# Scores of the remaining queries from six products instead of eight, with padded low keys filled by transfers and a new order of the work

## The chip, the core and the metric

The kernel runs on one core of a Trainium2 chip. The metric is the device time of one launch in microseconds (us); of the kernel before there are three runs: 879.49, 881.54 and 882.21 us, with the median 881.54. One more execution was recorded by the profiler: it took 880.19 us, 1.35 us less than that median, and 878.4 us of it are the span that the trace shows. Five engines work side by side on such a core: PE multiplies matrices (with PEld, its loading of weights, beside it), DVE, ACT and POOL work on vectors, and SP here only issues transfers (DMAs). Each takes its instructions in the order in which the program lists them, and waits at an instruction until what it reads is there and what it overwrites is free.

## What is computed

Thresholded attention over 8 batches of 8 heads with 576 positions of 64 numbers each, and behind it a gated MLP for each batch:

```python
scores = 0.125 * q @ k.T                          # 576 x 576 for each batch and head
thresh = scores.max(-1) - tau
attn = exp(where(scores >= thresh, scores, -1e9) - scores.max(-1))
x = (attn / attn.sum(-1)) @ v                     # heads side by side: 576 x 512 for each batch
h = gelu(x @ w_in)                                # 576 x 1024
u, g = h[..., :512], layernorm(h[..., 512:]) * g_ln
out = x + (u * (w_sg @ g + b_sg)) @ w_out
```

The large products are wanted at close to float32 precision. The kernel splits an operand into a high part (rounded to PE's fast format, fp32r) and a low part (the rest), and adds up high times high, low times high and high times low.

## The kernel before

**Pairs.** The 8 heads of a batch are worked in pairs, 64 rows of the 128 partitions for each head: 32 pairs, numbered n. Pairs 0 to 3 (the first batch, `whole_s`) take scores from unsplit operands. Pairs 4 to 31 (`by_rows`), with which the change deals, go by the split:

- `q_load` brings the queries of both heads (a tile rq), `q_scale` (POOL) multiplies them by 0.125, `q_hi` (ACT) writes the high part (qhi), `q_lo` (POOL) leaves the low part in rq. Four transfers (L472) build for each head h a tile qst[h]: the head's high queries in its own 64 rows, its low queries in the other 64.
- `k_load` brings the keys (rk), `k_hi` (ACT, L439) writes the high keys (khi, in the buffer that held qhi), four transfers (L456, `k_place`) put the high keys of head h into both halves of a tile ks[h], of which there are two sets for odd and even pairs.
- `k_lo` (POOL, L448) subtracts the high keys from the keys, once for each head, straight into klz[h]: a tile with the low keys of head h in its own 64 rows and zeros, written once at the start, in the other 64. There is one klz[0] and one klz[1] for all pairs.

So the product of qst[h] with ks[h] over 128 rows is high times high plus low times high, and that with klz[h] is high times low. `scores` (L546) makes a tile of 128 queries by 576 keys from them: two halves of 288 keys, two products each. A pair has nine tiles: four for each head, and between them one of the remaining 64 queries of both heads (i == NM, the tail tile). In the tail tile's columns of qst[0] the queries of head 1 are zeros, and the reverse; it sums both heads, four products for each half, eight in all.

**What follows a tile.** DVE takes the row maxima (L555, nm), POOL the threshold (L561), ACT the exponentials (L582, p or, for the tail tile, pm), DVE selects and sums (L589) and transposes blocks (L599, turned). When a pair is through, PE multiplies with the values v (L755). The inverse sums go out and back by transfers (L661 to L669, ld and ir); DVE scales (L762).

**MLP.** When four pairs are through, that batch's MLP products (L849) are mixed in between the scores of the next batch; the last batch's stand alone at the end. ACT changes its function table (L1164) whenever it goes from exponentials to gelu or back.

**Order.** Every step is put into a list by `at` or `put`. The table ORDER, a long string of numbers, says in which sequence the list is issued; each engine gets its instructions in that sequence. There is one such string for the kernel, written into it; FIRST_BANKS says which banks of PSUM the products use.

Of the kernel before, what the change touches and what calls it, by code (L numbers as in the profile page):

```python
# [37 lines left out]
    "G+zxNBj+qyd?xk4XF6bg3cEKMr!WF#YQ<7|Mnd5LDxOZmkA!nFj20*>?*+kq%I)dF{WXR6^uzQ0!7M6735qCfe0@#I>ZY^pz?wD&dREonuC{a2G)g_yc"
    "{o5FxPeAHEQ2{o3M`wJxiD>t-$B=V&pW&;GJ^3UyM<po5lG(6=egn`T(#9`7gMJ%T3<l4P8SuK<?{t(QNQO@gJXG%Hx@6;M+&gaA<`bTnYmSc__VF?1D"
    "zn6+rUO1ME%bcc1ix^%*sxCuDl-kH!T|-kO*dHJGCT&(62oQsoEDpqH^?zb&;<{sQ-(O7@(DzPZ(+zxM9_-K0e6K5VES#u&mV<tI?wNd{lzmb`9cf}0N"  # L40
    "p4F9<bCcHIfueyy1eOsr!QKzRjRd;sohNHrPc8;rK$UG%pxdIR4=FL5CE{Pyd4Z0Ta_D#f;Vr)L>GCWn=O|4}+VNE-HgnIEz#dvQP0OroyRK{JN1dojM"
    "ZYMxgkDH6ZaYs5sU2DW*lLV)HXVziu<dBre10mAEZmx6T&*!n{)a^oHsxOrK%vG;-Zfl{p{6MV;yU%}tC63vzURQMfdV#*kncv-uShB*>V~#r({Q-)JE"
# [70 lines left out]
Q = 32  # L113
# [9 lines left out]
def tile_threshold_attention_gated_mlp(  # L123
# [283 lines left out]
    def attention(n, g0):  # L407
# [34 lines left out]
        def k_part(h):  # L442
            return (S + front, 0) if h else (S, front)
# [728 lines left out]
```

## Time and profile before

| | before |
|---|---|
| runs, us | 879.49, 881.54, 882.21 (median 881.54) |
| profiled execution, us | 880.19, span 878.4 |
| busy in the span, us | PE 841.2, DVE 707.3, ACT 592.6, POOL 585.6 |
| granted clock of PE, mean | 0.996 |
| transfers | 117.00 MB, 46.5% of the 16 DMA engines' time |

The span has three stages. Until about 95 us the weights are split and pairs 0 to 3 run. From there to about 820 us attention of pairs 4 to 31 and the MLPs of the first seven batches run mixed. The last 58 us are the MLP of the last batch. Of a busy PE one must know that its matmuls overlap: a product of 288 columns is shown with about 0.3 us, but they start 0.13 us apart.

### The profile page before, as it was taken

How to read it: one execution, taken by the hardware profiler on the slowest of the kernel's cores; microseconds unless marked ns; L12 is line 12 of the kernel's file. 1: busy time of each engine (PE TensorE's matmuls, PEld its weight loads, DVE VectorE, ACT ScalarE, POOL GpSimd, SP SyncE). 2: the span in 40 equal slices, each digit the busy share in tenths (PEclk: the TensorE clock that was granted, in tenths of full speed). 3: DMA queues.
4: the chain of work that ended last, by engine and by line, in shares of the span. 5: the costliest groups of instructions: out<-in, count | busy, mean ns of one | idle time of the engine just before them, and what ended most of it. 6: DMA issues, size and time to landing. Idle time of an engine off the chain costs nothing.

```text
span 878.4 us, 30879 instructions
## 1 busy us (share of the span) xinstructions
PE 841.2 (96%) x12642; PEld 745.7 (85%) x12642; DVE 707.3 (81%) x1444; ACT 592.6 (67%) x1045; POOL 585.6 (67%) x965
## 2 busy tenths in 40 slices
PE   7998999989989999999999999999999999999998
PEld 4555789988878988898789988899889898999898
DVE  8998979888789889878888888898997888987111
ACT  6987986455865778755787657865677557784152
POOL 4875677575775576746776477755777667764477
PEclk9999999999999999999999999999999999999999
DMA  6642343475255464465555465356545545622101
GB/s 235 215 126 67 100 125 100 131 203 144 70 151 160 133 187 130 122 165 138 155 138 140 140 190 159 75 161 177 150 132 147 139 129 143 184 80 78 47 8 54
DMA packets 73024, 117.00 MB, mean 133 GB/s; under 512 B 10161, under 2 KB 32689, under 8 KB 72882
## 3 DMA queue, kind: packets, MB, share of 16 engines
q1 hardware_dynamic: 72882, 115.02, 46.5%
q8 instruction: 99, 1.62, 0.8%
q14 instruction: 43, 0.35, 0.1%
HBM read 70.55 MB, written 9.57 MB: 91 GB/s over the span
## 4 chain that ended last, share of the span: by engine, by line
PE 46%; POOL 13%; DVE 8%; ACT 5%; issue 5%; DMA 5%; SPq 1%; POOLq 0%; DVEq 0%; ACTq 0%
PE all_banks L849 29%; PE all_banks L546 9%; PE all_banks L755 7%; POOL ot L1056 3%; DVE nm L555 2%; DVE turned L599 2%; DVE p L589 2%; POOL klz L448 2%; ACT L1164 2%; DMA v<-in_vR 1%; POOL gl L1023 1%; POOL rq L465 1%; ACT p L582 1%; POOL vv L950 1%; POOL nm L561 1%
## 5 line engine op out<-in xcount | busy, mean ns | idle before, releaser
L582 ACT ACTIVATE p<-all_banks,nm 128x576 f32<-128x576 f32 x256 | 184.1, 737 | 110.4 <-DVE nm L555 109.3
L589 DVE SCALAR_TENSOR_TENSOR p<-all_banks,nm,p 128x576 f32<-128x576 f32 x256 | 202.1, 807 | 41.9 <-ACT p L582 25.1
L555 DVE TENSOR_REDUCE nm<-all_banks 128x1 f32<-128x576 f32 x288 | 207.0, 741 | 30.5 <-PE all_banks L546 22.2
L546 PE MATMUL all_banks<-ks,qst 128*128 128x288 f32 x560 | 164.2, 312 | 12.5 <-DVE p L589 7.4
L599 DVE STREAM_TRANSPOSE turned<-p 128x576 f32<-128x576 f32 x224 | 165.6, 756 | 2.2 <-PE all_banks L755 2.1
L546 PE MATMUL all_banks<-klz,qst 128*128 128x288 f32 x560 | 155.3, 296 | 3.3 <-POOL klz L448 2.7
L755 PE MATMUL all_banks<-turned,v 32*64 32x144 f32 x8064 | 147.1, 286 | 2.7 <-issue 1.7
L561 POOL TENSOR_TENSOR nm<-columns,nm 128x1 f32<-128x1 f32 x288 | 53.0, 192 | 133.7 <-DVE nm L555 112.8
L755 PEld LDWEIGHTS all_banks<-turned,v 32*64 32x64 f32 x8064 | 127.5, 130 | 16.3 <-issue 11.9
L546 PEld LDWEIGHTS all_banks<-ks,qst 128*128 128x128 f32 x560 | 105.1, 188 | 31.2 <-DVE p L589 18.4
L1164 ACT ACT_TABLE_LOAD x89 | 114.2, 1283 | 1.6
L849 PE MATMUL all_banks<-wsh,z 128*128 128x288 f32 (+2 forms) x512 | 110.7, 298 | 0.6 <-DVE p L589 0.6
L546 PEld LDWEIGHTS all_banks<-klz,qst 128*128 128x128 f32 x560 | 105.4, 188 | 5.2 <-POOL klz L448 4.0
L448 POOL TENSOR_TENSOR klz<-rk,khi 64x576 fp32r<-64x576 f32 x56 | 79.9, 1427 | 15.4 <-PE all_banks L546 8.4
L849 PEld LDWEIGHTS all_banks<-wsh,z 128*128 128x128 f32 x512 | 84.0, 188 | 2.7 <-DVE p L589 1.1
L849 PE MATMUL all_banks<-gh,woh 128*128 128x288 f32 (+2 forms) x256 | 75.9, 301 | 0.6 <-issue 0.2
L849 PE MATMUL all_banks<-xh,wih 128*128 128x288 f32 (+2 forms) x256 | 74.5, 298 | 0.6 <-DVE pm L589 0.4
L849 PE MATMUL all_banks<-gh,wol 128*128 128x288 f32 (+2 forms) x256 | 75.1, 298 | 0.0
L849 PE MATMUL all_banks<-xh,wil 128*128 128x288 f32 (+2 forms) x256 | 74.7, 298 | 0.0
L849 PE MATMUL all_banks<-xl,wih 128*128 128x288 f32 (+2 forms) x256 | 74.6, 295 | 0.0
L849 PE MATMUL all_banks<-wsl,z 128*128 128x288 f32 (+2 forms) x256 | 73.9, 296 | 0.0
L849 PE MATMUL all_banks<-gl,woh 128*128 128x288 f32 (+1 forms) x240 | 71.2, 300 | 0.0
(142 smaller groups left out, 1827.9 us busy)
## 6 DMA issues: line engine op xcount, KB each, us to landing
v<-in_vR SPq DMA_DIRECT2D x112, 288.0 KB
ks<-khi SPq DMA_DIRECT2D x112, 144.0 KB
rq<-in_qT SPq DMA_DIRECT2D x28, 320.0 KB
qst<-rq SPq DMA_DIRECT2D x56, 160.0 KB
qst<-qhi SPq DMA_DIRECT2D x56, 160.0 KB
rk<-in_kT SPq DMA_DIRECT2D x28, 288.0 KB
ir<-ld SPq DMA_DIRECT2D x56, 144.0 KB
out_T<-ot SPq DMA_DIRECT2D x56, 144.0 KB
```

The source lines that it names most:

```text
L448: nc.gpsimd.tensor_tensor(klz[h][rows, 0:w], st["k"][rows, o:o + w], st["kh"][rows, o:o + w], ALU.subtract)
L465: nc.gpsimd.tensor_tensor(lo.bitcast(F32R), lo, st["qh"][:, :wq], ALU.subtract)
L546: nc.tensor.matmul(sc[:, a, 0:HALF], w, x, start=(j == 0), stop=(j == len(terms) - 1))
L555: nc.vector.tensor_reduce(nmax, st["s", h, i][:, :, 0:HALF], AX.XY, ALU.max, negate=True)
L561: nc.gpsimd.tensor_tensor(thr, toff, st["nm", h, i], ALU.subtract)
L582: nc.scalar.activation(target(h, i), st["s", h, i][:, :, 0:HALF], AF.Exp, bias=st["nm", h, i])
L589: nc.vector.scalar_tensor_tensor(dst, st["s", h, i][:, :, 0:HALF], st["thr", h, i], dst, ALU.is_ge, ALU.mult, accum_out=st["l"][:, c:c + 1])
L599: nc.vector.transpose(st["turned"][:, :, o:o + Q], st["p", i][:, c0:c0 + S].rearrange("p (k x) -> p k x", x=Q))
L755: nc.tensor.matmul(st["accs"][g // 2][hs, g % 2, 0:W], st["v"][rows, o:o + D], st["turned"][rows, k, h * W:(h + 1) * W], start=(k == 0), s ...
L849: nc.tensor.matmul(st["acc"], *term(j), start=(j == 0), stop=(j == n - 1))
L1056: return lambda: nc.gpsimd.tensor_tensor(o(), o(), x[b, m][:, ts_], ALU.add)
L1164: tables[kind]()
```

## The change

The tail tile is made from three products for each half instead of four. The first two are high times high and low times high of head 0 and of head 1 (ks[0], ks[1]), as before. The two with zero padding are replaced by one: a new tile kl holds the low keys of both heads, each in its 64 rows, and a new tile qtail the high queries of the tail columns of both heads. Since the columns of one head are zeros in the other's rows, one product over 128 rows gives both.

- `k_lo` is one POOL subtraction over 128 rows into kl, instead of two over 64 rows into klz[0] and klz[1].
- klz[0] and klz[1], which the eight other tiles still need, are filled by two transfers from kl on SP's queue (`k_place_lo`, L449 of the kernel after).
- qtail is an ACT copy of 128 columns of qhi (`q_tail`, L453).
- kl and qtail are single buffers. kl of pair n+1 can be written when pair n's tail tile is through, and so can qtail. khi overwrites the buffer of qhi, so that khi of a pair now comes behind its qtail.
- The values of pairs 0 to 3 are loaded into a free part of the tile that later holds their transposed probabilities (tag pt), instead of a tile of their own.
- The host puts the tail columns of both heads last, and klz[1] is 576 wide instead of 640.
- ORDER and FIRST_BANKS are new: all engines get their work in another sequence. ACT has 79 changes of table in it, where it had 89 (the one at the start not counted).

```diff
--- before.py
+++ after.py
@@ -31,76 +31,77 @@
 ORDER = (
...
 FIRST_BANKS = (
...
@@ -226,7 +227,9 @@
     wt2 = cpool.tile([TAIL + 2, S], F32R, name="wt2")
 
     qst = [[cpool.tile([P, KW], F32R, name=f"qst{h}{i}") for i in range(2)] for h in range(2)]
-    klz = [cpool.tile([P, (S, KW)[h]], F32R, name=f"klz{h}") for h in range(2)]
+    klz = [cpool.tile([P, S], F32R, name=f"klz{h}") for h in range(2)]
+    kl = cpool.tile([P, S], F32R, name="kl")
+    qtail = cpool.tile([P, P], F32R, name="qtail")
     pm = cpool.tile([P, KW], F32, name="pm")
     nc.vector.memset(pm, 0.0)
 
@@ -417,9 +420,7 @@
         front = 0 if by_rows else TAIL
 
         def load(name, src, w):
-            if name == "v":
-                pool, width, tag = raws, KW, "v"
-            elif whole_s:
+            if whole_s:
                 pool, width, tag = {"q": ((raws, KW, "raw1"), (raws, S, "raw0"), (kpool, S, "ks01"), (xpool, S, "xl6")),
                                     "k": ((kpool, KW, "ks10"), (kpool, KW, "hi"), (kpool, KW, "ks11"), (xpool, KW, "xh6"))}[name][n]
             else:
@@ -439,22 +440,24 @@
                 nc.scalar.activation(st[name + "h"][:, :w], st[name][:, :w], AF.Copy)
             return f
 
-        def k_part(h):
-            return (S + front, 0) if h else (S, front)
-
-        def k_lo(h):
-            def f():
-                rows, (w, o) = slice(h * D, (h + 1) * D), k_part(h)
-                nc.gpsimd.tensor_tensor(klz[h][rows, 0:w], st["k"][rows, o:o + w], st["kh"][rows, o:o + w], ALU.subtract)
-            return f
+        def k_lo():
+            nc.gpsimd.tensor_tensor(kl, st["k"][:, 0:S], st["kh"][:, 0:S], ALU.subtract)
+
+        def k_place_lo(h):
+            def f():
+                rows = slice(h * D, (h + 1) * D)
+                nc.sync.dma_start(klz[h][rows].bitcast(F32), kl[rows].bitcast(F32))
+            return f
+
+        def q_tail():
+            nc.scalar.activation(qtail, st["qh"][:, MAIN:KW], AF.Copy)
 
         def k_place(h):
             def f():
-                w, o = k_part(h)
                 st["ks", h] = kpool.tile([P, (S, KW)[h]], F32R, tag=f"ks{h}{n % 2}", name=f"ks{n}_{h}")
                 for d0 in (0, D):
-                    nc.sync.dma_start(st["ks", h][d0:d0 + D, 0:w].bitcast(F32),
-                                      st["kh"][h * D:(h + 1) * D, o:o + w].bitcast(F32))
+                    nc.sync.dma_start(st["ks", h][d0:d0 + D, 0:S].bitcast(F32),
+                                      st["kh"][h * D:(h + 1) * D, 0:S].bitcast(F32))
             return f
 
         def q_scale():
@@ -468,13 +471,8 @@
             def f():
                 for h in range(2):
                     r0 = (h ^ swap) * D
-                    c0 = 0 if by_rows else h * TAIL
-                    nc.sync.dma_start(q[h][r0:r0 + D, c0:c0 + wq].bitcast(F32), st[name][h * D:(h + 1) * D, 0:wq].bitcast(F32))
-            return f
-
-        def q_zeros():
-            for h in range(2):
-                nc.gpsimd.memset(q[h][:, (S, 0)[h]:(KW, TAIL)[h]].bitcast(F32), 0.0)
+                    nc.sync.dma_start(q[h][r0:r0 + D].bitcast(F32), st[name][h * D:(h + 1) * D].bitcast(F32))
+            return f
 
         wq = KW if by_rows else S
         w = wq + (n == 0)
@@ -487,17 +485,22 @@
             at_k()
         else:
             at("q_hi", lead, hi_part("q", wq))
+            at("q_tail", lead, q_tail)
             at("q_lo", lead, q_lo)
             at("q_place", lead, q_place("qh", 0))
             at("q_place_lo", lead, q_place("q", 1))
-            if not by_rows:
-                at("q_zero", lead, q_zeros)
             at_k()
             at("k_hi", lead, hi_part("k", S + front))
+            at("k_lo", lead, k_lo)
             for h in range(2):
-                at("k_lo", lead, k_lo(h))
+                at("k_place_lo", lead, k_place_lo(h))
             at("k_place0", lead, k_place(0))
             at("k_place1", lead, k_place(1))
+
+        def rest_of(a, c0, w):
+            if ("half", a) not in st:
+                st["half", a] = ptp.tile([P, (NB * P, NB * 2 * W)[a]], F32, tag=("v4", "pt")[a], name=f"pt{n}_{a}")
+            return st["half", a][:, c0:c0 + w]
 
         def load_repeated(c):
             def f():
@@ -507,11 +510,15 @@
                 nc.sync.dma_start(st["v"][:, cs], vR[n - WHOLE_SCORES, :, cs])
             return f
 
+        def load_values():
+            st["v"] = rest_of(1, 9 * SPLIT[1][1], KW)
+            nc.sync.dma_start(st["v"], vP[b, hp])
+
         if by_rows:
             for c in range(NB * P // S):
                 at("v_load", g0, load_repeated(c))
         else:
-            at("v_load", g0, load("v", vP[b, hp], KW))
+            at("v_load", g0, load_values)
 
         def both_scores(i):
             def f():
@@ -529,19 +536,17 @@
             def f():
                 sc = st["s", h, i] = two_banks(f"s{n}_{h}_{i}")
                 for a in range(2):
-                    rows = slice(h * D, (h + 1) * D)
-                    qo, ko = h * 2 * TAIL + i * P, a * HALF
+                    cs, ks = slice(i * P, (i + 1) * P), slice(a * HALF, (a + 1) * HALF)
                     if whole_s and i == NM:
                         for g in range(2):
                             rows, qo = slice(g * D, (g + 1) * D), (1 - g) * MAIN
                             nc.tensor.matmul(sc[rows, a, 0:HALF], st["q"][rows, qo:qo + TAIL],
-                                             st["k"][rows, TAIL + ko:TAIL + ko + HALF], start=True, stop=True)
+                                             st["k"][rows, TAIL + a * HALF:TAIL + (a + 1) * HALF], start=True, stop=True)
                         continue
                     if i < NM:
-                        parts_of = [(h, q[h][:, qo:qo + P], ko)]
+                        terms = [(q[h][:, cs], x[:, ks]) for x in (st["ks", h], klz[h])]
                     else:
-                        parts_of = [(g, w, ko + g * front) for g, w in enumerate((q[0][:, MAIN:KW], q[1][:, 0:P]))]
-                    terms = [(w, x[:, o:o + HALF]) for g, w, o in parts_of for x in (st["ks", g], klz[g])]
+                        terms = [*((q[g][:, cs], st["ks", g][:, ks]) for g in range(2)), (qtail, kl[:, ks])]
                     for j, (w, x) in enumerate(terms):
                         nc.tensor.matmul(sc[:, a, 0:HALF], w, x, start=(j == 0), stop=(j == len(terms) - 1))
             return f
@@ -679,11 +684,6 @@
                         rows, c0 = slice(h * D, (h + 1) * D), h * TAIL
                         nc.scalar.activation(r[rows, MAIN:S], tp[rows, 1, c0:c0 + TAIL], AF.Copy)
             return f
-
-        def rest_of(a, c0, w):
-            if ("half", a) not in st:
-                st["half", a] = ptp.tile([P, (NB * P, NB * 2 * W)[a]], F32, tag=("v4", "pt")[a], name=f"pt{n}_{a}")
-            return st["half", a][:, c0:c0 + w]
 
         def unit(h, a):
             w = SPLIT[a][1]
@@ -1124,7 +1124,7 @@
             ends = np.zeros((d, groups, 2, half), q.dtype)
             ends[:, :, e] = x[:, rest[e]].reshape(d, groups, half)
             ends = ends.reshape(d, P)
-            qT[i, 2 * j + e, :, :wide] = np.concatenate([ends, x[:, body[e]]] if e else [x[:, body[e]], ends], axis=1)
+            qT[i, 2 * j + e, :, :wide] = np.concatenate([x[:, body[e]], ends], axis=1)
     vv = v.reshape(b, h // 2, 2, s, d)
     vm = np.ascontiguousarray(vv[:, :, :, :main].reshape(b, h // 2, 2, main // P, P, d).transpose(0, 1, 4, 3, 2, 5))
     vt = np.zeros((b, h // 2, 2, s - main, 2, d), v.dtype)
```

The order of the instructions shows the change at the transition from pair 17 to pair 18. In its names a number behind the name is that of the pair, with the head behind it or behind an underscore; the number behind the last underscore only tells buffers apart. qst00 and qst10 are qst of head 0 and 1 for even pairs, qst01 and qst11 those for odd ones; all_banks is PSUM.

On PE, pair 17's tail tile before:

```order
L546 MATMUL all_banks_93<-ks17_0_6247,qst01_136 128x288
L546 MATMUL all_banks_93<-klz0_139,qst01_136 128x288
L546 MATMUL all_banks_93<-ks17_1_6252,qst11_138 128x288
L546 MATMUL all_banks_93<-klz1_140,qst11_138 128x288
L546 MATMUL all_banks_93<-ks17_0_6247,qst01_136 128x288
L546 MATMUL all_banks_93<-klz0_139,qst01_136 128x288
L546 MATMUL all_banks_93<-ks17_1_6252,qst11_138 128x288
L546 MATMUL all_banks_93<-klz1_140,qst11_138 128x288
```

and after:

```order
L551 MATMUL all_banks_93<-ks17_0_6214,qst01_136 128x288
L551 MATMUL all_banks_93<-ks17_1_6211,qst11_138 128x288
L551 MATMUL all_banks_93<-kl_141,qtail_142 128x288
L551 MATMUL all_banks_93<-ks17_0_6214,qst01_136 128x288
L551 MATMUL all_banks_93<-ks17_1_6211,qst11_138 128x288
L551 MATMUL all_banks_93<-kl_141,qtail_142 128x288
```

Two products of the tile are gone. Behind it come other products, and then the tiles (0, 3) and (1, 3) of the pair, in both kernels.

On POOL, where pair 18's low keys are made (L561 and L566 are thresholds of pair 17, L950 a step of the MLP), before:

```order
L943 TENSOR_SCALAR bn3_3_6663<-bn3_3_6663 128x1
L448 TENSOR_TENSOR klz0_139<-rk18_6379,khi18_6490 64x576
L950 TENSOR_TENSOR vv3_3_6602<-vv3_3_6602,g_bc_108 128x512
L561 TENSOR_TENSOR nm17_1_3_6696<-columns_105,nm17_1_3_6696 128x1
L561 TENSOR_TENSOR nm17_0_3_6688<-columns_105,nm17_0_3_6688 128x1
L448 TENSOR_TENSOR klz1_140<-rk18_6379,khi18_6490 64x576
L619 TENSOR_SCALAR l17_6383<-l17_6383 128x9
```

and after:

```order
L566 TENSOR_TENSOR nm17_1_2_6613<-columns_105,nm17_1_2_6613 128x1
L444 TENSOR_TENSOR kl_141<-rk18_6208,khi18_6625 128x576
L950 TENSOR_TENSOR vv3_0_6347<-vv3_0_6347,g_bc_108 128x512
L566 TENSOR_TENSOR nm17_1_3_6686<-columns_105,nm17_1_3_6686 128x1
L566 TENSOR_TENSOR nm17_0_3_6678<-columns_105,nm17_0_3_6678 128x1
L963 TENSOR_TENSOR z3_0_6690<-vv3_0_6347,z3_0_6690 128x512
```

One subtraction stands where there were two, and it needs only the tail tile of pair 17 to be through, no longer the tiles (0, 3) and (1, 3).

On SP's queue, the transfers that put pair 18's keys into place (v4_17 are pieces of pair 17's values; rq19 and rk19 are loads of the next pair), before:

```order
L456 DMA ks18_1_6620<-khi18_6490 64x576 x2
L1059 DMA out_T<-ot2_1_1_6335 128x288
L1059 DMA out_T<-ot2_1_0_6227 128x288
L507 DMA v4_17_6625<-in_vR 128x576
L456 DMA ks18_0_6627<-khi18_6490 64x576 x2
L507 DMA v4_17_6625<-in_vR 128x576 x2
L431 DMA rk19_6816<-in_kT 128x576
```

and after:

```order
L459 DMA ks18_1_6666<-khi18_6625 64x576 x2
L510 DMA v4_17_6662<-in_vR 128x576
L459 DMA ks18_0_6670<-khi18_6625 64x576 x2
L449 DMA klz1_140<-kl_141 64x576
L449 DMA klz0_139<-kl_141 64x576
L432 DMA rk19_6700<-in_kT 128x576
L510 DMA v4_17_6662<-in_vR 128x576 x2
```

Two transfers that wait for pair 17's last tiles now stand in the queue, ahead of the load of rk19 and of two of the four pieces of pair 17's values.

## Rows read from the trace of the kernel before

**Rows 1.** Page: busy time (share of the span) and instructions of each engine.

```profile
PE 841.2 (96%) x12642; PEld 745.7 (85%) x12642; DVE 707.3 (81%) x1444; ACT 592.6 (67%) x1045; POOL 585.6 (67%) x965
```

**Rows 2.** Windows, mixed stage: busy us (instructions) of each engine, clock, DMA share, GB/s.

```profile
95.00:820.00 725.00, 702.34 (x11750) 640.73 (x11749) 613.93 (x1235) 493.58 (x833) 485.24 (x791) 1.00 0.51 139
```

**Rows 3.** Page, chain of work that ended last: shares of the span.

```profile
PE 46%; POOL 13%; DVE 8%; ACT 5%; issue 5%; DMA 5%; SPq 1%; POOLq 0%; DVEq 0%; ACTq 0%
PE all_banks L849 29%; PE all_banks L546 9%; PE all_banks L755 7%; POOL ot L1056 3%; DVE nm L555 2%; DVE turned L599 2%; DVE p L589 2%; POOL klz L448 2%; ACT L1164 2%; DMA v<-in_vR 1%; POOL gl L1023 1%; POOL rq L465 1%; ACT p L582 1%; POOL vv L950 1%; POOL nm L561 1%
```

**Rows 4.** Waits: us in total, times, longest.

```profile
DVE p L589 <- ACT p L582: 25.1, 36, 1.6
DVE nm L555 <- PE all_banks L546: 22.2, 36, 2.5
PEld all_banks L546 <- DVE p L589: 18.4, 44, 1.3
PEld all_banks L546 <- POOL klz L448: 4.0, 5, 2.2
PE all_banks L546 <- POOL klz L448: 2.7, 3, 2.0
```

**Rows 5.** Timeline of PE, pair 17's tail tile and four products ahead: start us, us, what.

```profile
438.36 0.29 PE L546 MATMUL all_banks<-ks,qst 128*128 128x288 f32 x1
...
439.81 0.30 PE L546 MATMUL all_banks<-klz,qst 128*128 128x288 f32 x1
439.94 0.29 PE L849 MATMUL all_banks<-gh,woh 128*128 128x288 f32 x1
```

**Rows 6.** Groups by line: busy us, mean ns of one, idle before, releasers.

```profile
L546 PE MATMUL all_banks<-ks,qst 128*128 128x288 f32 x560 | 164.2, 312 | 12.5 <-DVE p L589 7.4 <-DVE pm L589 2.1 <-DVE ir L762 1.1
L546 PE MATMUL all_banks<-klz,qst 128*128 128x288 f32 x560 | 155.3, 296 | 3.3 <-POOL klz L448 2.7 <-issue 0.5
L1164 ACT ACT_TABLE_LOAD x89 | 114.2, 1283 | 1.6
L448 POOL TENSOR_TENSOR klz<-rk,khi 64x576 fp32r<-64x576 f32 x56 | 79.9, 1427 | 15.4 <-PE all_banks L546 8.4 <-issue 2.3 <-DMA qst<-rq 1.4
L785 POOL TENSOR_TENSOR xl<-ir,xh 128x576 fp32r<-128x576 f32 x28 | 40.0, 1430 | 11.8 <-ACT xh L780 11.7
L1164 ACT ACTIVATE spare<-columns 128x1 f32<-128x1 f32 x89 | 18.1, 203 | 1.0
L730 ACT ACTIVATE pt<-all_banks 128x128 f32<-128x128 f32 (+1 forms) x20 | 5.5, 276 | 1.0 <-PE all_banks L242 0.8
```

**Rows 7.** Timeline of POOL, pair 18's low keys, and of DVE behind them.

```profile
443.92 1.43 POOL L448 TENSOR_TENSOR klz<-rk,khi 64x576 fp32r<-64x576 f32 x1 [0.65 <-PE all_banks L546]
445.30 1.29 POOL L950 TENSOR_TENSOR vv<-vv,g_bc 128x512 f32<-128x512 f32 x1
446.56 0.33 POOL L561 TENSOR_TENSOR nm<-columns,nm 128x1 f32<-128x1 f32 x2
446.96 1.44 POOL L448 TENSOR_TENSOR klz<-rk,khi 64x576 fp32r<-64x576 f32 x1
...
446.92 0.82 DVE L589 SCALAR_TENSOR_TENSOR p<-all_banks,nm,p 128x576 f32<-128x576 f32 x1 [0.21 <-POOL nm L561]
```

**Rows 8.** Timeline of PE: pair 17's last product with klz, pair 18's first two.

```profile
444.07 0.29 PE L546 MATMUL all_banks<-klz,qst 128*128 128x288 f32 x1
...
449.07 0.29 PE L546 MATMUL all_banks<-ks,qst 128*128 128x288 f32 x1
449.21 0.29 PE L546 MATMUL all_banks<-klz,qst 128*128 128x288 f32 x1
```

**Rows 9.** Issues of the key transfers on SP: ns min/median/max.

```profile
L456 SPq DMA_DIRECT2D ks<-khi x112: 461/593/1497, 80.0 to 768.3; - x112
```

**Rows 10.** Chain in order of time: transfers between tiles of SBUF, start us and us to landing.

```profile
261.19 2.61 DMA qst<-qhi
...
269.71 2.54 DMA ks<-khi
...
309.92 4.92 DMA qst<-rq
...
535.90 2.74 DMA qst<-rq
```

**Rows 11.** Timeline of ACT: the exponentials behind pair 17's tail tile.

```profile
440.64 1.35 ACT L582 ACTIVATE p<-all_banks,nm 128x576 f32<-128x576 f32 x2
```

**Rows 12.** Page: queue of the transfers: packets, MB, share of 16 engines.

```profile
q1 hardware_dynamic: 72882, 115.02, 46.5%
```

More of the change, by code (lines that the diff above doesn't have):

```diff
@@ L38 @@
[L38 to L42, printed above, removed]
@@ new lines @@
+    "1RNMx4yOZ<0w&yN)rD7FE;pt#2ZGNO5lHB4e<AKJKrBQ=J@fLotO9dtZBO^HfH#x2+5xi8^5vT#V%p(1p(!sEV!|6KH>%87a!XM6R$+uvEkrU^c()L$B"
+    "VH7<#W*&NDPMhhP^CA)`d+rgvg>v4cb%)!~wlbH2lC3BDgSY4lhWE2KZv&t|V^b6NMAt{=~SChw<%&Ku-80`U3982$ER{r-C!n&X~_eFk0ZW!NBl2`de"
+    "ZoUrLQf=G7|z#Rtm;3xfN#G^3voCm7lZScws!Ap*1+|17kbN*1&VX|_nstc61sHi+}ZkEPic1X>_00~RG@VP*`6KkznwAR<KsC-Ax0!f}qlU?nlZ;w#K"
+    "%j)w+lB_NzcqQVOg(js_q^JZ#LVh%Y;sg3YSf-vVtogu=I^YjwtmyJ>8LCiBqi4lnp7$gi7!$}(nq}jI+gdF}#<QhoEe6eyEC^dqU{4!enP|cD-j>#hN"
+    "4{8YIvo|+00}Bt?$h+AsnJJ6UEyOX4{E1a<Y4))*^H?P}2NyZwV}_uNy<shJJjvn?EL-d_@=m!!qu_iLSQnN4XJ7Gui{Q;}v!KFf;}br+`Ai%$b`>{w-"
@@ new lines @@
+    "fY1^v}f?lM*R7z+s(^`wV4$T2)!AUfHvT9SlIi?a8R>h!vMuI=f*ntbb;tLSR2Z5)p(rk)}3%c*@s)qquBKL^kG=MMSaRp9|uV?Y&abjsc^>tnRCI%kh"
+    "I-&D%erOJC~A8qJ~Go!C#hwu{+?}*!z6UC=<vnsX}ctHR6{9BWj!n{_Jp{OmtpxhSr>^M|Dfox3N-Dlc<cql~n36yM4vM*!qLz<a`SIp0U>4!qh_pafq"
+    "-H2?x1vo(!DiQ8_IS_piD|r`sqSYVZ`O7@@~dl@&D8j}b!v#>V4YyR0pWfZ3=X$?UHSLtH9~1nFRGluckGBAJHxDq^U}&4cr)|D?qS9Kj(&BabAWDH~$"
+    "uoRrX=Pc#k^l}glKc?_7%;?uYQ*pO6T!clN$!vItqP>n=!M5Bf|0f|3ze3e(c81(QijEj#-zT;jMOjxg()5XBCk7u4o#aVHtf#q+6&g{5__>&m6WcUbN"
+    "StK#csqz`^keDJ&CzbyT>?s0Upm{`(h?>Q1XeTmY@DsX8sxhe@SFV-EP?nQ7&NiMHt_shmag*}l@F4x?0LN`-VTk7ussA5OLSv&ycyyE{&L|V%O~_;v4"
@@ new lines @@
+    "TDzwtUaQT0`gH#o*{DYe86K!&b6mP1XUzb@)#SL>O=4dbjo2AP4#Qd#}&;Nr~j-q<dLYyC@yLU6-d3r2gTA-B~6hGN|HgwAZid0MKAKmQ>RhMP(ky7Qy"
+    "RDm8j(?>)_f&vEDqI3GPjd7sv1U;zphp0f%+0H6k`>|&=nq-Fjq7IieHMr_EAtUBuykt#GrT#wb+M9l<<X?8t<hNR{`}DWuno*G3j5$ymXm8HE=XOK?$"
+    "Tkus9e8_M<6+tKmuEblE&UpA#3lb66@2Bt=B8v2W}!df7jPi6%%>Dd3(DG8Z1z2#<$C{ih3UcR!VU6e-iG{VNCOr3wA0z>pXjsu}80;hPT_0E#hHV?Gq"
+    "FiK6+U!6!DC(!Z6c81XYR>PC@#l1L&^I+YBeB+bvBNup8FN!ulyhfjqr!m(d7pLanH=Ta7(B)AJ#lz)q&5>fMbIZGCxW@yjAM1;PA<!D?qZoq&Pp@k$0"
+    "Q?wPT%M3;_3YHJ+OdZPf6$M8nnFsBwQcZ~NqoVjF^bPom!a$?4PTO~hqLBQtae<i9R0u)+slzd<1$Gb~fvn4#B(+ak;1$YOiXzXxFnLk<we-!PqON%pM"
@@ new lines @@
+    "eyZPG3r`2I8a&h^@`eH1TY?12+P~;_PBO$TXLX;bz?PCoGghM*yN)+?-2@7MW=io=PEN+Y*<os-ytUURpwU`DzIURLE%i9yJa0>q5v=q4NHc_M}1Og?Q"
+    "VL$JaH0~K^ohQEFxi3ai-4UxNO25N9SS5EZ^wK5Q<OL{mWg@VyK)N=P2B8vGl+($callA|tapV<(GbF(1qkhZN9UM#fn-V5pH80UXdye959ykmKDVM1i"
+    "ey9<q^84$ZwWU1+;wRAA_`?<y-kxb8k#q;`8-V3sKS_Wz?2xP|)?9XLX1yK8#;m!`l?Kky~}&%1tLanQdnmB7mh4g9xGJLJE=p3y*g)4!jre+x}u5K7v"
+    "P$dg8Y6*4io@?Vd7HvyqR0CMa7zpnZf_Oyn;*x}2SRwdPSMt$S0)_0coCO5iYfy8DACOg0m&0r^u5E^lFNMY{>-1~0SC71OpjFfMOheRF8aJ7{7aNO=z"
+    ")^AKsP@7`E4E^eBI+uH*los|&Vw<bf(DLB6VClvX3RNV!!?+ofTd5<Wm6j_p*AiPABU(dDDcicq!3h<*n%s7tRD#{6)ZI)1{JGlEYtrPwKgUG621ezC9"
@@ L102 @@
[L102 to L103 removed]
+    "c-l3R2@=CF2m`tO{~vb+X)|_ef`kw@;}<m+S)KE0!aUMyUdB|1)vK-;Ypb>?5+iw8lE|t_x7cqTmFBE@4%VT4=2MXkKU|P-phT)<^YV#S5pRyLvs&9D&"
+    "jjMJhDH)So`kR<F@z49EvOuYE`dgYk*d%JXX=ZBZnZ1|0|7$-G8bb{yerQMp=u<^AOuP&bQE5zNhVCLqLo20xkk4n`<4{$6G@BZeI66-f0v2`&dtS?q1"
+    "2(SpFIjP3(25C8M1?km-0aJSB5b*TVn)61E$|5p(Y&6J77DmwMPG*`Z}>16cAsTmo$68WGZ02jD`OEVPfAX>|}1`o%41@ANWQfY{@jB1hCphvLr||)gG"
@@ L104 @@
+    "Q-M|&Uk(#XgCj<bC?Quj@5j9ih^?munV2qp"
 )
```

106 lines of the change are left out of this document (44 added, 62 removed).

## The prediction

> **What bounds the kernel now.** I read the busy times first, then those of the mixed stage, then the chain of waits, then the waits by name. The busy times put PE ahead with 96% and DVE second with 81% [rows 1]; in the mixed stage, where all of the change lies, PE is busy for 702.34 of 725 us and DVE for 613.93 [rows 2]. A busy PE is not one at its peak, since its products overlap: twelve of them start between 438.36 and 439.94 us, 0.132 us apart, while each is shown with 0.3 us [rows 5]. So PE has room that the 96% hides, and no engine alone sets the time. The chain says the same: 46% of it lies on PE, 13% on POOL, 8% on DVE, 5% each on ACT and on transfers [rows 3]. The waits are a ring: DVE waits for ACT's exponentials (25.1 us) and for PE's scores (22.2), PE for DVE to free a bank (18.4 us, the first line of it), and the scores for POOL's low keys (4.0 and 2.7) [rows 4]. A saving on one engine is worth its share of the chain, not its full size.
>
> **The change part by part**, against the profiled execution of 880.19 us, of which 878.4 are the span.
>
> *Two products for each half less.* 28 tail tiles lose two of their eight products, 56 in all. At 0.132 us from start to start [rows 5] that is 7.4 us of PE. The mean durations of 296 and 312 ns [rows 6] would make it 17, but they overlap. If only the part on the chain counts: the scores have 9% of the chain, 79 us [rows 3], and their 1120 products [rows 6] fill 1120 x 0.132 = 148 us, so 53%, and 3.9 us are saved. I take 7, near the upper end, since in the stage concerned PE is busy 97% of the time [rows 2] and what follows on it moves up; the range keeps 3.9 to 7.4.
>
> *One subtraction instead of two.* POOL did 56 subtractions of 1427 ns over 64 rows, 79.9 us. A subtraction of the same 576 columns over 128 rows takes 1430 ns [rows 6], so 28 x 1.43 = 40 us remain and 40 go. The subtraction has 2% of the chain, 17.6 us [rows 3]; half is 8.8 us. How it counts is seen at pair 18: POOL starts the first subtraction at 443.92, having waited for PE, goes on with a step of the MLP, and only then writes the thresholds at 446.56, for which DVE waits 0.21 us [rows 7]. What is late next are the other POOL steps in line, whose 1.29 us stay. Between 0 and 8.8 I take 5: the subtraction leaves the chain where it stood directly behind PE, and thresholds behind it come sooner, but DVE's own wait there was only 0.21 us.
>
> *The transfers into klz.* These replace POOL's write as the last step between a pair's last product with klz and the next pair's first one. At pair 17 that last product ends at 444.36 and the next pair's first score starts at 449.07: 4.7 us of other PE work cover it [rows 8]. Two issues of 0.593 us [rows 9] and a landing of 2.54 to 4.92 us (the four transfers between SBUF tiles that stand on the chain, three of them at or below 2.74 [rows 10]) make 3.7 to 6.1. So the usual landing is hidden with 1.0 us to spare, and the longest sticks out by 1.4. In the new order the products between the two, counted and taken at their spacings, are worth 1.7 us at one transition (pair 7 to 8), 4.1 to 4.8 at four and 5.6 to 9.3 at the other 22. With the usual landing only the first is short, by 2.0 us; with the longest, the short ones add up to about 12. I take 3 and keep 0 to 12. The Trainium skill ("DMA: Bandwidth & Descriptors", section on the anatomy of one DMA) gives some 2.0 us plus the bytes at 436 GB/s, for its other way of issuing; for 147,456 bytes an estimate from it is 2.3 us. The shortest landing here, 2.54 us [rows 10], is longer; by the page's price this term would be 1.8 instead of 3.
>
> Behind the waiting transfers on SP's queue stand the next key load, two pieces of this pair's values and then the inverse sums: a late klz also holds up L755. What hides that is that the values are needed only after DVE's transposes; if that cover is gone, it costs the same microsecond again, inside the 12. The transfers add 56 x 144 KB = 8.3 MB to 115.02, so the queue's share of 46.5% [rows 12] becomes about 50%; transfers have 5% of the chain, 44 us [rows 3], and 7% more of it would be 3 us. I take 0 for that and keep 3.
>
> *ACT.* 28 copies of 128 columns for qtail at some 0.276 us (an eviction of that width [rows 6]) add 7.7 us; ten changes of table less, each 1.283 + 0.203 us [rows 6], take off 14.9. The table loads have 2% of the chain, 17.6 us [rows 3], ten of 89 of it 2.0; ACT's 5% of the chain over 592.6 us busy [rows 1, 3] makes the copies worth 0.6. I take 1, from -0.6 to 2. Now the next pair's khi waits in ACT's queue behind qtail, and that for PE's tail tile; behind them stands an exponential that DVE waits for. The cover: the tail tile's products ended at 440.1 [rows 5], before the exponentials that follow it started at 440.64 [rows 11], so ACT arrives later than PE. Without it, each of 28 would hold up an exponential.
>
> *What costs nothing.* The values of pairs 0 to 3 go to another tile that is freed by the same product as before; the host's layout is outside the metric; the narrower klz[1] shortens one write at the start.
>
> *The new order.* No row of before prices it. DVE is idle for 725 - 613.93 = 111 us of the mixed stage [rows 2]; another sequence may give back or take a tenth of that, 11 us, either way. I take 0.
>
> The sum: -7 - 5 + 3 - 1 = -10 us, so 870.2 us for an execution like the profiled one, and 871.5 against the median of 881.54.
>
> **The rivals.**
>
> *The full gain.* PE's 7.4, POOL's 8.8 and ACT's 2.0 all reach the end, the transfers stay hidden, and with 40 us less on POOL the thresholds come earlier all along, so that a part of DVE's 111 us of idle time closes too, some 3 us: -21, 860 us. For it: POOL holds 13% of the chain [rows 3]. Against: PE's banks wait for DVE, which loses no work.
>
> *DVE takes over.* What PE and POOL save turns into waits for DVE, whose 707.3 us [rows 1] are untouched; the 18.4 us [rows 4] that PE waits for DVE's select grow by what PE saved. Only POOL's wait of the scores, 6.7 us [rows 4], is to be had, less the 3 for transfers and up to 3 for their traffic: 880. For it: DVE is busy 85% of the mixed stage [rows 2]. Against: DVE itself waits for ACT and PE for 47 us [rows 4].
>
> *The transfers become the link*, the one that ends slower. At each of 28 transitions klz lands behind four key transfers and pieces of the values issued just ahead on the same queue. With 4.7 us of cover and 1.2 for the issues it decides from a landing of 3.5 us; the gain of 13 is eaten at 13/28 = 0.46 us more, 4.0 us; a landing of 4.5 costs 28 x 1.0 = 28 us: 881.5 - 13 + 28 = 896. For it: one of the four landings was 4.92 us [rows 10]. Against: three were at most 2.74, and the count of the new order's products leaves 5.6 us or more at 22 transitions. The same page's rules for kernel authors say that two transfers to disjoint halves of the partitions are not worth splitting, since they share the same engines and serialize; klz[0] and klz[1] are such a pair. By that the second lands later than one issue behind the first, which is this rival's mechanism; no row of before shows two such transfers alone.
>
> *ACT's gate.* qtail finds the tail tile unfinished and holds up an exponential of 0.7 us at each of 28 pairs: +20 - 13, 888 us. The row on the cover speaks against it.
>
> **How the numbers follow.** The forecast, 866 to 877, has a chance of 0.48; the full gain 0.20; DVE taking over 0.18; the transfers 0.10; ACT's gate 0.04. A measurement of this kernel can tell about 0.3% from no change, 2.6 us. Faster by more than that are the forecast, the full gain and a little of the third: 0.72. The third, the two edges beside it included, gives 0.13 within 0.3%. Slower are the last two and the third's upper edge: 0.15. The range goes from 857, the full gain with the new order's luck, to 884, where the third case meets 2.5 us of late transfers; about 0.03 lies below it and 0.14 above.
>
> **What would show it right or wrong.** Right: 1064 score products; the subtraction as 28 of about 1.43 us and POOL busy near 546 us; waits of the scores for the klz transfers under 5 us in total; ACT near 585 us; the gain spread over the mixed stage, none of it in the first 95 or the last 58 us. Wrong: waits of PE for klz transfers of 10 us or more, or landings above 4 us, speak for the third rival; an unchanged idle time of DVE with more waits of PE for DVE's select for the second; a longer first or last stage for the order alone.

## The result, and the profile after

The changed kernel takes 875.8 us, the median of 13 runs (868.19 to 879.82), against 882.58 for the kernel before in the same comparison (13 runs, 879.49 to 884.6): a ratio of 0.9914, with an interval of 0.989 to 0.9939, so some 7.6 us less. The forecast was 871.5 us, 10 us less, in a range of 857 to 884. Sign and range held; the gain is three quarters of what was forecast. The profiled execution took 871.83 us, of which 870.0 are the span; that is 4 us below its median, which must be kept in mind where the traces are set side by side.

The page of the kernel after: busy time, queue of the transfers, chain of the work that ended last by engine.

```profile
PE 830.4 (95%) x12586; PEld 735.8 (85%) x12586; DVE 707.6 (81%) x1444; ACT 584.3 (67%) x1053; POOL 547.6 (63%) x937
q1 hardware_dynamic: 77362, 123.29, 50.5%
PE 43%; DVE 18%; POOL 14%; ACT 9%; issue 8%; DMA 6%; SPq 1%; POOLq 0%; DVEq 0%; ACTq 0%
```

Against [rows 1], PE has 56 products and 10.8 us less, POOL 38.0 us, ACT 8.3; DVE is untouched. The three parts of the span, cut at the first and last product with klz, in the columns of [rows 2], first before and then after:

```profile
0.00:93.20 93.20, 82.57 (x515) 51.44 (x516) 83.15 (x186) 76.14 (x163) 58.99 (x121) 0.98 0.46 152
93.20:802.80 709.60, 686.94 (x11386) 625.98 (x11385) 609.22 (x1226) 489.17 (x825) 475.41 (x775) 1.00 0.51 140
802.80:878.40 75.60, 71.74 (x746) 68.26 (x744) 14.89 (x34) 27.32 (x58) 51.24 (x71) 0.99 0.15 50
```

```profile
0.00:91.70 91.70, 81.99 (x515) 49.95 (x516) 83.51 (x187) 74.84 (x163) 59.91 (x121) 1.00 0.53 167
91.70:793.00 701.30, 675.90 (x11324) 616.97 (x11323) 609.08 (x1225) 482.18 (x833) 438.34 (x748) 1.00 0.55 152
793.00:870.00 77.00, 72.48 (x752) 68.90 (x750) 15.03 (x34) 27.32 (x58) 49.30 (x68) 0.99 0.14 43
```

The mixed stage is 8.3 us shorter, the one before it 1.5 us, the one behind it 1.4 us longer. What was changed shows in the groups by line and in the waits (us in total, times, longest), in this order: the subtraction, the products with klz, the copy for qtail; then the waits of PE for the transfers and for DVE's select, of ACT's copy for the tail tile, of DVE for scores and exponentials.

```profile
L444 POOL TENSOR_TENSOR kl<-rk,khi 128x576 fp32r<-128x576 f32 x28 | 40.1, 1434 | 18.8 <-ACT khi L440 17.6 <-DMA v<-in_vR 1.2
L551 PE MATMUL all_banks<-klz,qst 128*128 128x288 f32 x448 | 124.6, 295 | 0.8 <-DMA klz<-kl 0.4
...
PEld all_banks L551 <- DMA klz<-kl: 1.1, 2, 0.7
PE all_banks L551 <- DMA klz<-kl: 0.4, 1, 0.4
PEld all_banks L551 <- DVE p L594: 17.0, 41, 1.0
ACT qtail L453 <- PE all_banks L551: 16.8, 7, 3.5
DVE nm L560 <- PE all_banks L551: 16.9, 31, 2.6
DVE p L594 <- ACT p L587: 24.6, 41, 1.9
```

PEld and PE often show the same standstill, once each: a product and its weights wait together. So of two such lines only the longer one counts. Against [rows 4], 4.0 us of waiting for POOL's low keys have become 1.1 us for the transfers, PE waits no more for DVE than before (17.0 against 18.4), and DVE waits 5.3 us less for scores. ACT does wait for the tail tile, in seven places. On the chain DVE has 18% where it had 8% [rows 3], and 17 to 20% in four more executions (the changed kernel again, twice with a second qtail, once without the transfers); yet DVE's idle time in the mixed stage fell from 100.4 to 92.2 us.

### The profile page after: what moved, and what is told of

Its sections match the earlier page's. It is cut to its first block, busy times and chain, and to the rows that moved or that the text cites. A ratio compares the mean times of both kernels' runs of the same rounds, so it can differ in the third digit from the quotient of the medians.

```text
span 870.0 us, 30824 instructions
## 1 busy us (share of the span) xinstructions
PE 830.4 (95%) x12586; PEld 735.8 (85%) x12586; DVE 707.6 (81%) x1444; ACT 584.3 (67%) x1053; POOL 547.6 (63%) x937
## 3 DMA queue, kind: packets, MB, share of 16 engines
q1 hardware_dynamic: 77362, 123.29, 50.5%
## 4 chain that ended last, share of the span: by engine, by line
PE 43%; DVE 18%; POOL 14%; ACT 9%; issue 8%; DMA 6%; SPq 1%; POOLq 0%; DVEq 0%; ACTq 0%
PE all_banks L849 26%; PE all_banks L551 8%; PE all_banks L755 6%; DVE p L594 5%; DVE nm L560 5%; DVE turned L604 4%; ACT p L587 2%; POOL ot L1056 2%; DMA qst<-qhi 2%; POOL vv L950 2%; POOL gl L1023 1%; POOL z L963 1%; POOL nm L566 1%; DMA ir<-ld 1%; DMA klz<-kl 1%
## 5 line engine op out<-in xcount | busy, mean ns | idle before, releaser
L551 PE MATMUL all_banks<-ks,qst 128*128 128x288 f32 x560 | 156.8, 313 | 13.1 <-DVE p L594 6.5
L755 PEld LDWEIGHTS all_banks<-turned,v 32*64 32x64 f32 x8064 | 127.9, 130 | 19.2 <-issue 17.2
L566 POOL TENSOR_TENSOR nm<-columns,nm 128x1 f32<-128x1 f32 x288 | 53.4, 191 | 137.2 <-DVE nm L560 115.0
L551 PEld LDWEIGHTS all_banks<-ks,qst 128*128 128x128 f32 x560 | 101.6, 188 | 31.8 <-DVE p L594 17.0
L551 PE MATMUL all_banks<-klz,qst 128*128 128x288 f32 x448 | 124.6, 295 | 0.8 <-DMA klz<-kl 0.4
L551 PEld LDWEIGHTS all_banks<-klz,qst 128*128 128x128 f32 x448 | 84.3, 188 | 2.5 <-DMA klz<-kl 1.1
L849 PE MATMUL all_banks<-wih,xh 128*128 128x512 f32 x160 | 63.2, 396 | 0.5 <-ACT uu L838 0.4
```

What stands on the lines that cost most here:

```text
L551: nc.tensor.matmul(sc[:, a, 0:HALF], w, x, start=(j == 0), stop=(j == len(terms) - 1))
L566: nc.gpsimd.tensor_tensor(thr, toff, st["nm", h, i], ALU.subtract)
L755: nc.tensor.matmul(st["accs"][g // 2][hs, g % 2, 0:W], st["v"][rows, o:o + D], st["turned"][rows, k, h * W:(h + 1) * W], start=(k == 0), s ...
L849: nc.tensor.matmul(st["acc"], *term(j), start=(j == 0), stop=(j == n - 1))
```

## The experiments

The kernel before ran beside each of them on the same chip (880.96 to 881.84 us, 9 to 26 runs a chip).

**Eight products in the new order.** Only the terms of the tail tile are put back; kl, qtail, the transfers and the order stay (L551, the line of the six products).

```diff
-terms = [*((q[g][:, cs], st["ks", g][:, ks]) for g in range(2)), (qtail, kl[:, ks])]
+terms = [(q[g][:, cs], x[:, ks]) for g in range(2) for x in (st["ks", g], klz[g])]
```

> The kernel after with the tail tile made from eight products again (ks and klz of both heads); kl, qtail, the transfers and the new order stay. Theory of the prediction: the 56 products are worth 7 us, so this run loses them, about 882 us, level with the kernel before. Rival (DVE takes over): PE has slack, the products cost nothing at the end, 875 to 877. Between them, the chain's share of the scores: 879 to 880.

Measured: 889.08 us, 1.01 of the kernel before (1.0076 to 1.0124), some 16 us above the changed kernel by the two ratios. All three expectations are missed: 56 products of 0.132 us cost twice their own time. Where the rest comes from is found below.

**Copies on POOL in place of the transfers.** The change itself, but klz is filled by POOL from kl.

```diff
-nc.sync.dma_start(klz[h][rows].bitcast(F32), kl[rows].bitcast(F32))
+nc.gpsimd.tensor_scalar(klz[h][rows], kl[rows], 1.0, 0.0, ALU.mult, ALU.add)
```

> The kernel after with the two transfers into klz replaced by two POOL copies from kl over 64 rows, at the same places of the order; POOL does about 40 us more, as much as before the change. Theory of the prediction: POOL's 5 us come back and the transfers' 3 us go, about 878. Rival (the transfers are the price of the change): they held back several us, 870. Rival (POOL is what matters, since a copy that waits for PE stands ahead of the thresholds): 885 or more.

Measured: 891.43 us, 1.0121 (1.0099 to 1.0143). POOL is busy 584.4 us, as before the change, and half of the 36.8 us that it has more reach the end. Its waits show where some of that goes: the copy is the last step ahead of a pair's first product, and 11.1 us are waited for it in 14 places (the second line is the same standstills at the product itself).

```profile
PEld all_banks L551 <- POOL klz L449: 11.1, 14, 1.6
PE all_banks L551 <- POOL klz L449: 7.7, 8, 1.4
```

**A second tile for qtail.** ACT's copy then needs no longer wait for the previous pair's tail tile. It ran twice, the second time beside the changed kernel itself.

```diff
-qtail = cpool.tile([P, P], F32R, name="qtail")
+qtails = [cpool.tile([P, P], F32R, name="qtail"), tail_b]
...
+qtail = qtails[n % 2]
```

> The kernel after with two buffers for qtail, for odd and even pairs, so that ACT's copy no longer waits for the tail tile of the pair before (16.8 us of ACT idle in seven places after the change); the unit matrix sum both lies in the second buffer's room, and the keys of pair 2 in another tile. Theory of the prediction: the gate costs nothing, since other waits end later, 875 to 877. Rival (ACT's gate): each of the seven waits holds up exponentials, and 5 to 10 us come back, 866 to 871.

> The changed kernel as it is, beside the next three on one chip, so that they have a common base. Expected about 875.8 us, 0.991 of the kernel before, with runs spread over some 10 us.

> A second tile for qtail again, now beside the changed kernel itself. If ACT's wait for the tail tile (16.8 us in seven waits) were on the path, it would be 8 us or more faster than the changed kernel, 868. If it lies beside other work, the two agree within 2 us, with less scatter at most.

Measured: 871.93 us, 0.9906 (0.9891 to 0.9922), in the first run, between the two theories and without the changed kernel beside it. In the second the changed kernel took 872.07, 0.9908 (0.9875 to 0.9941), and the one with two tiles 873.34, 0.9922 (0.9895 to 0.9949). The seven waits are real and cost nothing that can be measured here.

**The work of the changed kernel in the order of before**, with a second qtail; the transfers are issued where POOL's two subtractions stood.

```diff
 ORDER = (the table of before)
...
-at("k_lo", lead, k_lo)
-for h in range(2):
-    at("k_place_lo", lead, k_place_lo(h))
+for h in range(2):
+    at("k_lo", lead, k_lo_of(h))    # the subtraction at the first, a transfer at each
```

> The work of the kernel after in the order of the kernel before: six products, kl, qtail (two buffers, copied directly ahead of the high keys), transfers into klz issued where POOL's two subtractions stood; 89 changes of table. Theory of the prediction: the work makes the gain and the order is worth about 0 and one us of ACT, so 872 to 877. Rival (the order makes the gain): 880 to 884. Rival (the transfers need an order that was made for them): above 884, with waits of PE for klz transfers.

Measured: 968.11 us, 1.099 (1.0974 to 1.1005). Of the 87 us above the kernel before, 53.4 are one wait, in 19 places that both lines show; with it the mean granted clock fell to 0.963 (0.996 before), and the ends of pages, found below, took 14.2 us. What the rest is made of stays open.

```profile
PEld all_banks L562 <- DMA klz<-kl: 53.4, 19, 7.1
PE all_banks L562 <- DMA klz<-kl: 49.0, 19, 6.8
```

**The price of the transfers in the new order**: left out at all pairs but the first, and issued twice.

```diff
+if n == WHOLE_SCORES:
     nc.sync.dma_start(klz[h][rows].bitcast(F32), kl[rows].bitcast(F32))
```

> Leaves out the two transfers into klz at all pairs but the first split one, so that the low keys in klz are stale; all else as the changed kernel. It shows what the transfers still cost. My prediction's term (+3, from 0 to 12) gives 873 from 876. If they are hidden and their traffic costs nothing: 875 to 876. If their place on the queue and their traffic hold up the key loads and the values as well: 866 or less.

> Every transfer into klz is issued twice, all else as the changed kernel: the queue is held for about 1.2 us more at each transition, the second pair lands some 1 to 2 us later. If the cover in the new order is ample (5.6 us or more at 22 of 28 transitions), 876 to 880. If the cover is used up, each of 28 transitions pays 1 us or more: 904 or more.

Measured: without them 873.29 us, 0.9922 (0.9894 to 0.995), no different from the changed kernel beside it (872.07; the 873 expected was counted from 876); twice, 980.28 us, 1.1128 (1.1098 to 1.1158), 3.9 us for each of 28 transitions. The second transfer writes what the first one writes, so SP's queue stands still until the first has landed (first line; L450 is the doubled issue), twice at each transition, and then PE waits (62.6 us in 30 places; the last two lines are the same standstills):

```profile
SPq L450 <- DMA klz<-kl: 142.4, 56, 4.8
...
PEld all_banks L552 <- DMA klz<-kl: 62.6, 30, 4.9
PE all_banks L552 <- DMA klz<-kl: 55.4, 28, 4.7
```

So the edit does not put the second pair 1 to 2 us later, as expected, but holds the queue for two more landings in a row, 5.1 us at each transition. PE stands still for 2.2 us of them. The mean granted clock was 0.957 there, 0.998 in the changed kernel beside it, so that not all of the 3.9 us is this wait. One pair of transfers is hidden; two more landings in a row are not.

**The relief in the order of before.** Three kernels in that order, without transfers and qtail: six products, one subtraction, and both.

```diff
-terms = [(w, x[:, o:o + HALF]) for g, w, o in parts_of for x in (st["ks", g], klz[g])]
+terms = [(w, x[:, o:o + HALF]) for g, w, o in parts_of for x in (st["ks", g], klz[g])][:2 if i < NM else 3]
...
+if h == 0 or n == WHOLE_SCORES:
     nc.gpsimd.tensor_tensor(klz[h][rows, 0:w], st["k"][rows, o:o + w], st["kh"][rows, o:o + w], ALU.subtract)
```

> The kernel before, in its own order, with six products in the tail tile: the one of klz[1] is left out in both halves, so head 1's high times low is missing from the tail tile's scores. It prices the 56 products alone, without transfers and without the new order. My prediction's term is 7 us (3.9 to 7.4): 874, bounds 873.9 to 877.4. If they are worth what putting them back into the new order cost (13 to 17 us): 864 to 868. If they stand beside waits: 880.

> The kernel before, in its own order, with one of the two low-key subtractions left out (klz[1] is written at the first split pair alone, its low keys are stale afterwards): 27 steps of POOL of 1.43 us less, eight products stay. It prices POOL's relief alone. My prediction's term is 5 us (0 to 8.8): 876. If POOL's relief is worth what two copies on POOL cost in the new order (15 us for 56 of them, some 7 for half): 874. If only the waits of the scores for it are to be had: 878 or more.

> Both together in the order of before: six products in the tail tile (head 1's high times low left out there) and one subtraction instead of two (stale low keys in klz[1]), no transfers into klz, no qtail. It shows what the relief alone gives without a new order. By the sum of my terms (7 and 5): 869.5. If the old order can't use the relief, 876 or more, and the new order is what brings it in. If the changed kernel loses something by its order or transfers: 864 or less.

Measured: six products 886.56 us, 1.0061 (1.0037 to 1.0086); one subtraction 877.59, 0.9957 (0.9938 to 0.9975); both 882.78, 1.0012 (0.9992 to 1.0032). POOL's relief is worth 4.2 us. Taking 56 products away makes the kernel 5 us slower, with two subtractions as with one. The waits that the profile calls "issue" (the engine waited for nothing that the profile shows) tell where, in PE's products with the values, for before, for six products, and for eight in the new order (here too PE's line shows standstills of PEld's once more):

```profile
PEld all_banks L755 <- issue: 11.9, 58, 1.0
PE all_banks L755 <- issue: 1.7, 3, 0.8
```

```profile
PEld all_banks L755 <- issue: 20.5, 68, 2.1
PE all_banks L755 <- issue: 7.9, 12, 1.8
```

```profile
PEld all_banks L755 <- issue: 26.4, 72, 1.8
PE all_banks L755 <- issue: 12.6, 15, 1.5
```

The same block of 192 such products, once in before and once with six products in the tail tile (timeline of PE: start us, us, what):

```profile
606.67 1.04 PE L755 MATMUL all_banks<-turned,v 32*64 32x144 f32 x48
608.05 2.51 PE L755 MATMUL all_banks<-turned,v 32*64 32x144 f32 x144 [0.33 <-DMA v<-in_vR]
610.49 0.40 PE L546 MATMUL all_banks<-ks,qst 128*128 128x288 f32 x1
```

```profile
605.43 2.22 PE L755 MATMUL all_banks<-turned,v 32*64 32x144 f32 x122
609.47 1.45 PE L755 MATMUL all_banks<-turned,v 32*64 32x144 f32 x70 [1.83 <-issue]
610.85 0.54 PE L546 MATMUL all_banks<-ks,qst 128*128 128x288 f32 x1
```

In the second PE stops for 1.83 us in the middle of the block, with its operands there. What it waits for is its own instructions. They arrive by a queue that the page lists (packets, MB, share), 16 KB at a time:

```profile
q8 instruction: 99, 1.62, 0.8%
```

PE's trace of before has 25,438 instructions (each product, each loading of weights, the semaphores), some 257 for each of the 99 packets. I numbered them in the order of the trace and looked at every gap of over 0.25 us from start to start between two neighbouring products with the values:

```text
kernel                          gaps at 192 to 195 of 256   elsewhere     pages done in under 2.6 us
before                             4, 2.9 us                1, 0.6 us            0
before, one subtraction            4, 2.2                   0                    0
before, six products              13, 11.6                  2, 0.8               5
before, both                      13, 12.3                  0                    6
changed kernel (first, second)     8, 6.5; 8, 6.2           0; 1, 0.3            0; 0
changed, eight products           16, 17.2                  1, 0.5              13
work of after, order of before    13, 14.2                  1, 1.6               9
```

The gaps lie at one place of each stretch of 256 instructions, a page (it begins where some 63 instructions ahead of the first one of the trace would have it), and in every one of these PE goes on 0.95 to 1.7 us after a packet of that queue has landed. So PE waits at the end of a page that ran off faster than the next one could be brought. That happens behind slower pages too: in the first execution of the changed kernel no page was through in less than 2.85 us, and eight ended in a gap. Products of 288 columns take 0.132 us with their weights [rows 5], those with the values about 0.02 us, so a page made of these alone is through in 2 us. A block has 384 instructions: whether a whole page falls into it depends on where the page begins, and four instructions less for each of 28 pairs move that. The Trainium skill ("Runtime: NRT & Kernel Launch", section "Instruction fetch mechanics") says that instructions come in blocks of 16 KiB, 256 instructions each, by a DMA queue of the sequencer, and that this is mostly hidden, since instructions are issued more slowly than they are brought. The trace agrees on the blocks (99 packets of 16 KB); for pages of small products it is not hidden here (2.9 to 17.2 us in the table).

**Six products, with the pages where they were.** The two products left out become small ones of the form of those with the values, so that PE has as many instructions as before.

```diff
+if i == NM and j == 2:
+    nc.tensor.matmul(sc[0:64, a, 0:144], w[0:32, 0:64], x[0:32, 0:144], start=False, stop=False)
```

> The kernel before in its own order with six full products in the tail tile; the two products that the run with six left out stand there as small ones instead (32 rows, 64 x 144, like those with the values; they multiply zeros, so head 1's high times low is missing from the tail tile's scores as there). PE gets as many instructions as in the kernel before, so that every page of 256 instructions in PE's stream begins where it began there, while nearly all of the work of the 56 products is gone. If the run with six lost its gain to waits for PE's own instructions, which moved with the stream: the waits of the products with the values for issue go back from 28 us to about 13, and the time is 0.991 to 0.993 of the kernel before, 874 to 876. If the work of the 56 products is worth nothing in the old order, or taking it away makes other waits: 881 to 887, like the run with six.

Measured: 891.8 us, 1.0115 (1.0095 to 1.0136). The waits went back as the first theory says (below, L760 is the line of the products with the values; by the count above 4 gaps of 3.3 us at the ends of pages, where six products had 13 of 11.6), and yet the time rose. The cause is in the tail tile itself (L549 is the small product):

```profile
PEld all_banks L760 <- issue: 11.5, 53, 1.3
PE all_banks L760 <- issue: 2.1, 3, 1.1
...
444.74 0.29 PE L551 MATMUL all_banks<-klz,qst 128*128 128x288 f32 x1
444.96 0.28 PE L549 MATMUL all_banks<-klz,qst 32*64 32x144 f32 x1
445.17 0.40 PE L551 MATMUL all_banks<-ks,qst 128*128 128x288 f32 x1
445.41 0.29 PE L854 MATMUL all_banks<-gh,woh 128*128 128x288 f32 x1
```

From one start to the next it is 0.22, 0.21 and 0.24 us around a small product, where full ones follow in 0.132: some 0.27 us more than three full spacings (over all 56 the medians are 0.22, 0.21 and 0.24), 15 us for 56, against 10.2 us measured above the kernel before. So the filler cost more than what it replaced. That the ends of the pages make the waits is shown by where they stand in every stream of instructions tried, and by their going when the pages went back; how much of the time they make is not, by this run.

## Why the prediction was right, point by point

**Two products less: 7 us.** The work is worth about that, but the edit had a second effect that the sum lacked. Set the profiled executions side by side and take off what the ends of the pages took and what the granted clock took (1 minus its mean, times the time). Six products in the order of before against before: +5.7 measured, of it 11.6 - 2.9 = 8.7 for the pages and 3.0 for the clock (0.9922 against 0.9955), so the products gave 6.0. Both against one subtraction alone: +0.1, of it 10.1 for the pages and -3.6 for the clock (0.9922 against 0.9881), so the products gave 6.4. Eight in the new order against six: 15.4 (887.25 against 871.83), of it 10.7 for the pages, so 4.7. The three, 4.7 to 6.4, lie in the bounds of 3.9 to 7.4. This is an account and no proof. It assumes that both reach the end whole, and the run with small products speaks against that: there 15 us for these, 0.4 for the pages and 1.2 for the clock make 16.7, where 11.6 were measured between the profiled executions. And each figure is from one execution, while runs of the changed kernel with the same mean clock of 0.997 lie up to 8.8 us apart. What failed is not the size of the term but that the list of what the change moves left out PE's own instructions, worth up to 14 us (2.9 against 17.2).

**One subtraction instead of two: 5 us.** 4.2 measured in the order of before, with bounds of 0 to 8.8. The step counted as foretold: 28 of 1434 ns, POOL at 547.6 us. How much such a step is worth depends on where it stands: two copies, 36.8 us of POOL in place of the 38.6 taken away here, cost four times as much in the new order, where they stand ahead of a pair's first product. Why the gain in the order of before is small is not shown by that, since the subtraction that was left stands there too: PE still waits 2.6 us for it, where it was 4.0 [rows 4].

**The transfers: 3 us.** They cost nothing that can be measured: left out, the time is the same within the 3 us or so by which these runs scatter. The count of the cover, 5.6 us or more at 22 of 28 transitions, is borne out: PE waits 1.1 us in all, in two places. Landings above 4 us, named as a sign against it, do occur (one of 4.57 us is even on the chain), but PE never waits more than 0.7 us for one. The 3 us for traffic were rightly left out of the sum, though the queue's share rose from 46.5% [rows 12] to 50.5%.

**ACT: 1 us.** Busy 584.3 against "near 585". The cover named, that ACT comes later than PE, fails at seven pairs, and still nothing is lost, as the second qtail shows. What the ten changes of table gave was not measured by itself.

**The new order: 0, give or take 11.** This was the term with the least behind it, and it carries the result. Without it the change costs 10% (transfers) or nothing is gained (both reliefs, 1.0012). With it the transfers are hidden, and the waits at the ends of pages are 6.5 us instead of 12.3. Taking the rest of the profiled executions together: -5.7 (products, mean of the three), -4.2 (POOL), +3.6 (pages, 6.5 against 2.9), -1.8 (clock, 0.9976 against 0.9955) make -8.1; measured were -8.4. The 4.2 us are a difference of medians; by the account of the profiled executions POOL's part is 6.0 (880.02 against 880.19 us, clock 0.9881, pages 2.2), and the sum -9.9. So for the order itself, apart from making the transfers and the pages fit, between 0.3 us gained and 1.5 us lost is left, which is less than the scatter. No run has the whole old work in the new order; with half of it put back (eight products, or the copies on POOL) that order was 1% slower than the kernel before, which speaks against a gain by the order alone.

**What was luck.** The sum came near, -10 against -7.6, in part because two errors cancel: the 3 us put down for the transfers are not there, and 3.6 us at the ends of pages, which were not in the sum, are.

**The rivals.** DVE did not take over: PE's waits for its select fell, and so did DVE's idle time, though DVE's share of the chain rose. The 6.7 us that this rival counts for POOL's low keys are standstills of 4.0 us, seen on PEld and again on PE. The full gain did not come: the subtraction gave 4 to 6 us instead of 8.8, and the pages took 3.6. The transfers as the link, 896, were a matter of the order alone: in the order of before they are that link, at 968, worse than this rival had it; single waits reach 7.1 us. ACT's gate is there and costs nothing.

## What to carry to other kernels

Work taken from the busiest engine was worth most of its start-to-start time here, but only in an order made for what is left: judge such an edit with and without a new order before calling it useless. A transfer in place of a step on a vector engine was free here as long as its landing fitted between the last reader and the next one, and cost dearly beyond that. Where an engine runs hundreds of very short instructions in a row, any edit that changes the number of its instructions, even far away, can move time between runs of the same work: look at the waits for issue and at where they stand in the stream.

## What the hardware showed that I had not expected

- PE's own instructions can run out. A page of 256 is brought while the one before runs; pages through in 2.0 to 2.1 us ended in gaps of 0.24 to 1.82 us (changed kernel with eight products), and in every gap over 0.25 us there PE went on 0.95 to 1.7 us after the packet had landed.
- A single small product (32 x 64 rows and columns) between full ones costs more than a full one: three spacings of 0.21 to 0.24 us instead of 0.132.
- A subtraction of 576 columns on POOL takes as long over 128 rows (1434 ns) as over 64 [rows 6].
- The changed kernel's 13 runs lie 11.6 us apart, those of before 5.1. A part goes with the granted clock: in the twelve runs of the kernel with one subtraction the seven with a mean of 0.992 or more took 875.05 to 877.66 us and the five below it 878.98 to 881.72. In the changed kernel the tie is looser (868.19 to 876.98 us at 0.997), and what else scatters it stays open.
